# Decode attention on one core: the output projection's weights loaded as 112 + 12 rows instead of 128

## The chip, the cores and the metric

The kernel runs on one core of a Trainium2 chip. The metric is device time in microseconds of one execution, and the median over several runs is given. Besides there is one execution taken by the hardware profiler, whose span runs from the first to the last instruction.

## What is computed

A single token goes through layer norm, attention over a cache of 32,768 keys and values for each of 32 heads, an output projection, a residual, and then a dense block with the activation mish. Everything is in bf16.

```python
B, Sq, D = 1, 1, 512
H, Sk, Dh = 32, 32768, 128          # dense block: F = 1376
q = (layernorm(x) @ wq).reshape(B, Sq, H, Dh).transpose(0, 2, 1, 3)
scores = einsum("bhqd,bhkd->bhqk", q, k_cache) * Dh ** -0.5
o = einsum("bhqk,bhkd->bhqd", softmax(scores), v_cache)
h = x + o.transpose(0, 2, 1, 3).reshape(B, Sq, H * Dh) @ wo      # wo: [4096, 512]
z = layernorm(h) @ w1 + b1
h2 = h + (z * tanh(softplus(z))) @ w2
```

The caches of keys and values are 256 MB each; all weights together are some 11 MB.

## The kernel before

*Order of the loads.* All bulk loads are issued by SP, in one order written out by hand: wq, the keys of head 0, then for each head its keys and the values of the head before it, then `WO` (the output projection's weights wo), the values of the last head `("v", 31)` in five pieces, `WL` (wo's 128 rows for the last head alone), four pieces of w1 and four of w2. Before a load SP waits until the tile it fills has been read (`freed_by`, `done_with`). A load increments a semaphore by 16 when it has landed; `ready[slot]` counts the loads into a slot of the ring, and `ready_wait` turns the count in `fills` into the value to wait for. `start` issues one load.

*Buffers.* `ring` is one large tile of 128 partitions and six slots of 32 KB per partition. One head's keys or values take two slots: 256 positions for each partition, 64 KB. wo takes one slot, viewed as `wo_v` with 32 rows of wo, that is 32 KB, on each partition: partition p holds the rows 32p to 32p+31. Since a head has 128 rows, head h lies on the partitions 4h to 4h+3, and the last head's on 124 to 127.

*One head.* PE transposes 128 x 128 blocks of keys into PSUM (line 685), DVE copies them to `ering` (L691), PE multiplies them with the query (L661). The softmax follows with its maximum and sum over the partitions (`soft_a`, `soft_b`, `soft_exp`, `soft_c`), then PE multiplies the values with the probabilities (L712) and DVE scales the result into a column of `oT` (L720). The heads run as a loop, so that head h's values are used while the keys of head h+1 are transposed.

*The end.* `mid` runs once the second last head is done: the heads' outputs, without the last head's, are transposed into `oX`, whose rows for the last head are zero, and 32 matmuls (L798) contract `oX` with `wo_v`; their results are summed up into `yps` (L803). Then the last head's values arrive in five pieces and PE takes them one after another; `project_last` adds that head's part with `WL` (L779). In `tail` the second layer norm, w1 (L834), mish and w2 (L854) follow, and SP stores the result (L589).

The lines that the change touches are the count of `fills`, the load of wo, and the operands of the 32 matmuls.

Of the kernel before, what the change touches and what calls it, by code (L numbers as in the profile page):

```python
# [13 lines left out]
PE, ACT, DVE, POOL, SP = "pe", "act", "dve", "pool", "sp"  # L14
# [293 lines left out]
def build_kernel(nc, A_x, A_k_cache, A_v_cache, A_wq, A_wo, B_w1, B_b1, B_w2, out):  # L308
    D = A_x.shape[-1]
    Dh = 128  # L310
    HD = A_wq.shape[1]
    H = HD // Dh
# [29 lines left out]
    def sb(shape, dt, name):  # L342
        cm = nc.sbuf_tensor(name, shape, dt)
        t = cm.__enter__()
        allocs.append(cm)
        return t.ap()

    def ps(shape, name, dt=F32):
        cm = nc.psum_tensor(name, shape, dt)
        t = cm.__enter__()  # L350
        allocs.append(cm)
        return t.ap()
# [23 lines left out]
    oX = sb([128, 64], BF16, "oX")  # L376
# [14 lines left out]
    T_f = [ps([128, GT * 64], f"tps{i}") for i in range(NT)]  # L391
# [21 lines left out]
    ready = [sem(f"ready{i}") for i in range(NS)]  # L413
# [3 lines left out]
    s_out = sem("s_out")  # L417
    WQ, WO, WL = ("wq",), ("wo",), ("wl",)
    W1P = [("w1", n) for n in range(KC)]

    W2_J = [0, 4, 8, FJ]
    W2P = [("w2", n) for n in range(len(W2_J))]
# [6 lines left out]
    def pieces(what):  # L429
        kind, h = what  # L430
        if what in (("k", 0), ("v", H - 1)):
            at = CUTS[kind]
        else:
            at = [TPS] if what in (("k", 1), ("v", 1)) else [64] if what == ("k", H - 1) else []
        return list(zip([0] + at, at + [SCOLS]))
# [4 lines left out]
    def uncut(what):  # L440


        kind, h = what
        for r in CUTS[kind]:
            if not cut_at(kind, h, r) and (h == 0 or cut_at(kind, h - 1, r)):
                n = 1
                while h + n < H and not cut_at(kind, h + n, r):
                    n += 1
                yield r, n

    def later_k(h):

        if h == 2:
            for r in CUTS["k"]:
                yield r, sum(1 for n in range(1, H) if n == 1 or not cut_at("k", n, r))

    order = [WQ, ("k", 0)]
    for h in range(1, H):
        order += [("k", h), ("v", h - 1)]
    order += [WO, ("v", H - 1), WL] + W1P + W2P  # L460
    cut_sems = {k: {r: sem(f"cut_{k}_{r}") for r in CUTS[k]} for k in CUTS}

    s_wl = sem("wl")
    s_k1 = sem("k1")
    w1_sems = [sem(f"w1_{n}") for n in range(len(W1P))]
    w2_sems = [sem(f"w2_{n}") for n in range(len(W2P))]
# [6 lines left out]
    def slot_of(what):  # L473
        if what in HOMES:
            return HOMES[what]
        if what[0] in ("w1", "w2"):
            return HOMES[WL]
        return V_HOME if what[0] == "v" else what[1] % 2 * HALVES

    fills = {}  # L480
    for what in order:
        if what[0] in ("k", "v") or what in (WQ, WO):
            fills[what] = 1 + sum(1 for x in fills if slot_of(x) == slot_of(what))

    def ready_wait(what):
        if what == WL:
            return (s_wl, 16)
        return (ready[slot_of(what)], 16 * fills[what])
# [4 lines left out]
    def freed_by(what):  # L493
        if what == WO:
            return done_with("k", H - 2, 0, SCOLS)
        if what[0] == "k" and what[1] > 1:
            return done_with("k", what[1] - 2, 0, SCOLS)
        if what == ("v", 0):
            return [free_name(WQ)]
        return []  # L500

    def tiles_of(what):
        return ring[:, slot_of(what):slot_of(what) + HALVES, :].rearrange("p s (r d) -> p (s r) d", d=Dh)

    def keys_of(cache, h):
        return cache[0, h, :, :].rearrange("(p r) d -> p r d", r=SCOLS)

    wq_v = ring[:, slot_of(("wq",)), :].rearrange("p (k n) -> p k n", k=KC)
    wo_v = ring[:, slot_of(("wo",)), :].rearrange("p (j n) -> p j n", j=32)
# [6 lines left out]
    def done_with(kind, h, r0, r1):  # L516
        if kind == "v":
            return [f"pv{h}_{r1}" if r1 in V_EVENTS else f"pv{h}"]
        return [free_name(("k", h, half)) for half in range(HALVES) if r0 < (half + 1) * TPS and r1 > half * TPS]
# [15 lines left out]
    def program(S):  # L535
        S.home_bytes = HALVES * SLOT * 2
        t_ = nc.tensor
# [6 lines left out]
        def start(dst, src, s):  # L544
            S.dma(SP, lambda: sp.dma_start(dst, src).then_inc(s, 16))  # L545
# [3 lines left out]
        for what in order:  # L549
            slot = slot_of(what)  # L550
            if what == ("k", 1):
                S.stay(SP)
            S.wait(SP, freed_by(what))
            flat = ring[:, slot, :]
            if what[0] == "wq":
                S.wait(SP, ["b1z"])
                start(b1r[0:FJ // 2, :], B_b1[0:FJ * 128].rearrange("(i p) -> i p", i=FJ // 2), s_b1)
                start(b1r[FJ // 2:FJ // 2 + 1, 0:FLAST], B_b1[FJ * 128:F].rearrange("(o p) -> o p", o=1), s_b1)
            elif what[0] == "wo":
                start(flat, A_wo.rearrange("(p j) n -> p (j n)", j=32), ready[slot])  # L560
            elif what == WL:
                start(wol_v, A_wo[(H - 1) * Dh:H * Dh, :], s_wl)
            elif what[0] == "w1":
                k = what[1]
                start(w1_v[:, k, :], B_w1[k * 128:(k + 1) * 128, :], w1_sems[k])
            elif what[0] == "w2":
                n = what[1]
                if n + 1 < len(W2_J):
                    j0, j1 = W2_J[n], W2_J[n + 1]
                    start(w2_v[:, j0:j1, :].rearrange("p (i s) n -> p i (s n)", s=2),  # L570
                          B_w2[j0 * 128:j1 * 128, :].rearrange("(i p s) n -> p i (s n)", p=128, s=2), w2_sems[n])
                else:
                    start(w2_v[0:FLAST, FJ, :], B_w2[FJ * 128:F, :], w2_sems[n])
            else:
                kind, h = what
                rows = keys_of(A_k_cache if kind == "k" else A_v_cache, h)
                for r0, r1 in pieces(what):
                    if kind == "v" and h:
                        S.wait(SP, done_with(kind, h - 1, r0, r1))
                    if what == ("k", 1):  # L580
                        s = ready[slot] if r0 else s_k1
                    else:
                        s = cut_sems[kind][r0] if r0 else ready[slot]
                    start(tiles_of(what)[:, r0:r1, :], rows[:, r0:r1, :], s)


                for r, n in uncut(what) if kind == "v" else later_k(h):
                    S.dma(SP, lambda r=r, n=n: sp.sem_inc(cut_sems[kind][r], 16 * n))
# [194 lines left out]
        def mid():  # L783
            n_b1 = FJ // 2 + 1
            for s in range(2):
                S.step(PE, lambda s=s: t_.matmul(B1_PAIRS[:, s, :], b1r[:, :].rearrange("i (q s) -> i s q", s=2)[:, s, :],
                                                 identb[0:n_b1, 0:FJ // 2], start=True, stop=True),
                       waits=([(s_b1, 32)] if s == 0 else ()))
            S.step(PE, lambda: t_.matmul(B1_REG[:, FJ:FJ + 1], b1r[:, 0:128], identb[0:n_b1, FJ // 2:n_b1], start=True, stop=True),
                   name="b1t")  # L790
            S.step(ACT, lambda: a.copy(b1c[:, :], B1_REG), name="b1c", waits=["b1t"])
            S.step(DVE, lambda: v.transpose(oZ[:, :], oT[:, :]), name="oZ", waits=[f"oev{H - 2}", "oTz"])
            S.step(PE, lambda: t_.matmul(OX_PS, perm[:, :], oZ[:, :], start=True, stop=True), name="oXs", waits=["oZ", "perm"])
            S.step(DVE, lambda: v.tensor_copy(oX[:, 0:32], OX_PS), name="oX", waits=["oXs"])


            for j in range(32):
                S.step(PE, lambda j=j: t_.matmul(T_f[1][32 * (j % 4):32 * (j % 4 + 1), 0:D], oX[:, j:j + 32], wo_v[:, j, :],  # L798
                                                 start=(j < 4), stop=(j >= 28), skip_group_check=True),
                       name=("yrow" if j == 31 else None), waits=(["oX", "oXz", ready_wait(("wo",))] if j == 0 else ()))  # L800
            S.step(DVE, lambda: v.tensor_copy(yrow[:, :], T_f[1][:, 0:D]), name="yrs", waits=["yrow"])
            for c in range(KC):
                S.step(PE, lambda c=c: t_.matmul(yps[:, c:c + 1], yrow[:, c * 128:(c + 1) * 128], sel[:, :],  # L803
                                                 start=(c == 0), stop=False, skip_group_check=True),
                       waits=(["yrs", "sel"] if c == 0 else ()))

        def tail():
# [54 lines left out]
            S.stayed(ACT)  # L862

        S.rounds(H, head, turn, rest, mid, tail)

    log = {}
# [42 lines left out]
```

## Time and profile before

| | |
|---|---|
| median of 3 runs | 1275.37 us (1275.34 to 1275.58) |
| span of the profiled execution | 1273.6 us |
| busy PE / DVE / ACT / POOL | 80% / 56% / 2% / 0% |
| read from HBM | 548.21 MB |
| wo's load, from its issue to its landing | 35.6 us |

The profiled execution's own time beside its span is not listed; the median of the runs lies 1.8 us above the span, which counts from the first to the last instruction only. Shares of busy time are averages over the span. A load's packet is here one partition's row of that load; a window's DMA share and rate count the packets that start in it, so a share can come out a little over 1. "SPq" is SP's queue of issues. In a chain, a time in "DMA" is what passed from the issue to the landing of a load.

### The profile page before, as it was taken

Reading aid. Unit: us, or ns where it says so; the run is one execution under the profiler, and the core shown is the slowest. Engines: PE = TensorE matmul, PEld = TensorE weight load, DVE = VectorE, ACT = ScalarE, POOL = GpSimd, SP = SyncE. Lnnn points to the kernel's source line nnn. Section 1 sums busy time; section 2 is a strip of 40 time slices with the busy share of each in tenths; the row PEclk is TensorE's granted clock in tenths of the full one; section 3 lists DMA queues with packets and bytes.
Section 4 is the critical chain, followed back from the end, with each engine's and each line's share of the span. In section 5 each row is a group of like instructions: output and inputs, shape, how many; then the busy total and the mean of one; then the engine's idle time right before and its main releaser. Section 6 shows DMA issues by size and latency. Waiting matters only on the chain.

```text
span 1273.6 us, 54445 instructions
## 1 busy us (share of the span) xinstructions
PE 1016.5 (80%) x25046; PEld 988.9 (78%) x25046; DVE 715.8 (56%) x1252; ACT 20.6 (2%) x71; POOL 0.9 (0%) x8
## 2 busy tenths in 40 slices
PE   4689877779777789777788777797777897777995
PEld 4689877779777789777788777797777887777994
DVE  2566664456654466644466644566544666445661
ACT  0000000000000000000000000000000000000000
POOL 0000000000000000000000000000000000000000
PEclk9888876778877688867788776787777887677885
DMA  9999999999999999999999999999999999999998
GB/s 403 445 417 437 432 438 434 440 428 428 432 438 430 445 428 428 430 440 428 445 430 428 430 438 430 440 434 428 428 438 432 434 440 428 428 436 434 426 435 353
DMA packets 12350, 548.35 MB, mean 431 GB/s; under 512 B 1360, under 2 KB 1590, under 8 KB 2998
## 3 DMA queue, kind: packets, MB, share of 16 engines
q1 hardware_dynamic: 12340, 548.22, 99.7%
q8 instruction: 8, 0.13, 0.0%
q10 hardware_dynamic: 2, 0.00, 0.0%
HBM read 548.21 MB, written 0.00 MB: 430 GB/s over the span
## 4 chain that ended last, share of the span: by engine, by line
DMA 54%; DVE 23%; PE 18%; issue 2%; SPq 2%; POOL 0%; POOLq 0%
DMA ring<-in_A_k_cache_dram 51%; DVE ering L691 23%; PE ops L712 9%; PE tps L685 6%; DMA ring<-in_A_v_cache_dram 2%; SPq L545 2%; PE sps L661 1%; DMA ring<-in_B_w_dram 1%; PE hlp L736 1%; PE hlp L731 1%; PE hlp L746 0%; PE tps L854 0%; DVE pmax L725 0%; DVE perm L859 0%; DVE gmax L733 0%
## 5 line engine op out<-in xcount | busy, mean ns | idle before, releaser
L685 PE MATMUL tps<-identb,ring 128*128 128x128 bf16 x8192 | 668.3, 232 | 209.4 <-DMA ring<-in_A_k_cache_dram 204.9
L691 DVE COPY ering<-tps 128x1024 bf16<-128x1024 bf16 x1024 | 669.4, 692 | 259.7 <-PE tps L685 258.5
L685 PEld LDWEIGHTS tps<-identb,ring 128*128 x8192 | 522.2, 104 | 212.2 <-issue 212.2
L661 PE MATMUL sps<-qcur,ering 128*128 128x1 bf16 x8192 | 343.7, 164 | 7.7 <-DVE ering L691 6.7
L661 PEld LDWEIGHTS sps<-qcur,ering 128*128 128x128 bf16 x8192 | 309.2, 97 | 10.7 <-DVE ering L691 9.4
L712 PEld LDWEIGHTS ops<-pbuf,ring 128*128 128x128 bf16 x8192 | 226.3, 103 | 24.4 <-issue 15.1
L712 PE MATMUL ops<-pbuf,ring 128*128 128x1 bf16 x8192 | 231.3, 165 | 10.8 <-DMA ring<-in_A_v_cache_dram 8.3
L720 DVE TENSOR_TENSOR oT<-ops,rtotc 128x1 f32 x31 | 5.0, 162 | 109.8 <-PE ops L712 109.8
L733 DVE TENSOR_REDUCE gmax<-hlp 1x1 f32<-1x128 f32 x32 | 8.9, 278 | 67.5 <-PE hlp L731 67.5
L738 DVE TENSOR_SCALAR nbias<-hlp 128x1 f32<-128x1 f32 x32 | 5.1, 158 | 63.4 <-PE hlp L736 63.4
L741 ACT ACTIVATE pbuf<-sps,nbias 128x256 bf16<-128x256 f32 x32 | 15.2, 474 | 1219.9 <-PE ops L712 1166.7
L731 PE MATMUL hlp<-ident,pmax 128*1 128x128 f32 x64 | 17.9, 379 | 5.2 <-issue 5.2
L725 DVE TENSOR_REDUCE pmax<-sps 128x1 f32<-128x256 f32 x32 | 13.6, 425 | 14.3 <-PE sps L661 14.3
L736 PE MATMUL hlp<-gmax,onesmat 1*128 1x1 f32 x64 | 18.5, 356 | 0.4 <-DVE gmax L733 0.4
L736 PEld LDWEIGHTS hlp<-gmax,onesmat 1*128 1x128 f32 x64 | 15.8, 304 | 1.3 <-DVE gmax L733 0.9
L746 PE MATMUL hlp<-esum,onesmat 128*128 128x1 f32 x64 | 12.1, 258 | 4.8 <-issue 1.0
L746 PEld LDWEIGHTS hlp<-esum,onesmat 128*128 128x128 f32 x64 | 9.5, 188 | 7.4 <-issue 7.4
L640 PE MATMUL hlp<-xnT,ring 128*128 128x1 bf16 x128 | 3.6, 165 | 9.2 <-DMA ring<-in_A_wq_dram 9.2
L640 PEld LDWEIGHTS hlp<-xnT,ring 128*128 128x128 bf16 x128 | 3.5, 104 | 9.3 <-issue 9.3
L720 DVE TENSOR_TENSOR oL<-ops,rtotc 128x1 bf16<-128x1 f32 x1 | 0.2, 161 | 14.3 <-PE ops L712 14.3
L731 PEld LDWEIGHTS hlp<-ident,pmax 128*1 128x1 f32 x64 | 2.8, 81 | 5.8 <-issue 5.3
L748 DVE RECIPROCAL rtotc<-hlp 128x1 f32<-128x1 f32 x32 | 5.4, 168 | 2.7 <-PE hlp L746 1.4
(77 smaller groups left out, 40.1 us busy)
## 6 DMA issues: line engine op xcount, KB each, us to landing
ring<-in_A_k_cache_dram SPq DMA_DIRECT2D x3, 4096.0 KB, 40.2
ring<-in_A_v_cache_dram SPq DMA_DIRECT2D x3, 4096.0 KB, 15.3
ring<-in_A_k_cache_dram SPq DMA_DIRECT2D x3, 2048.0 KB, 30.5
ring<-in_A_k_cache_dram SPq DMA_DIRECT2D x1, 6144.0 KB, 44.6
ring<-in_A_wq_dram SPq DMA_DIRECT2D x1, 4096.0 KB, 12.2
ring<-in_A_wo_dram SPq DMA_DIRECT2D x1, 4096.0 KB, 35.6
ring<-in_A_v_cache_dram SPq DMA_DIRECT2D x1, 2048.0 KB, 16.1
ring<-in_B_w_dram SPq DMA_DIRECT2D x4, 344.0 KB, 20.7
```

The costliest lines, as they stand in the source:

```text
L545: S.dma(SP, lambda: sp.dma_start(dst, src).then_inc(s, 16))
L640: S.step(PE, lambda h=h, kc=kc: t_.matmul(Q_REG[:, h:h + 1], wq_v[:, kc, h * Dh:(h + 1) * Dh], xnT[:, 0, kc:kc + 1], start=(kc == 0), stop ...
L661: S.step(PE, lambda r=r: t_.matmul(S_ps[:, col0 + r:col0 + r + 1], ering[:, bg % NE, r, :], qcur[:, :], start=True, stop=True), name=(name ...
L685: S.step(PE, lambda r=r, at=at: t_.matmul(tb[:, r * 128:(r + 1) * 128], key_tile(S, at), identb[:, :], is_transpose=True, start=True, stop ...
L691: S.step(DVE, lambda: v.tensor_copy(ering[:, bg % NE, :, :].rearrange("p r d -> p (r d)"), tb[:, :]), name=f"ev{bg}", waits=[f"trb{bg}"], ...
L712: S.step(PE, lambda r=r: t_.matmul(o_ps[:, 0:1], vt[:, r, :], pbuf[:, r:r + 1], start=(r == 0), stop=(r == SCOLS - 1)), name=(names or Non ...
L725: S.step(DVE, lambda: v.tensor_reduce(pmax[:, :], S_ps[:, 0:SCOLS], AXX, ALU.max), name=f"pmax{h}", waits=[f"qkh{h}"], kind="pmax")
L731: S.step(PE, lambda: t_.matmul(A_REG, pmax[:, :], ident[:, :], start=True, stop=True), name=f"A{h}", waits=[f"pmax{h}", "ident", f"rcp{h - ...
L733: S.step(DVE, lambda: v.tensor_reduce(gmax[:, :], A_REG, AXX, ALU.max), name=f"gmax{h}", waits=[f"A{h}"], kind="gmax")
L736: S.step(PE, lambda: t_.matmul(B_REG, onesm[0:1, :], gmax[:, :], start=True, stop=True), name=f"B{h}", waits=[f"gmax{h}", "consts0"] + ([] ...
L741: S.step(ACT, lambda: a.activation(pbuf[:, :], S_ps[:, 0:SCOLS], ACTF.Exp, bias=nb[:, :], scale=SC, accum_out=esum[:, :]), name=f"exp{h}", ...
L746: S.step(PE, lambda: t_.matmul(C_REG, onesm[:, :], esum[:, :], start=True, stop=True), name=f"C{h}", waits=[f"exp{h}"], kind="C")
```

## The change

The rows of the last head on the partitions 124 to 127, which meet zeros in `oX`, are no longer loaded into `wo_v`. The remaining 124 partitions come in five loads: partitions 0 to 111 with whole rows of 32 KB; partitions 112 to 123 with the first 22 of their 32 rows of wo (22 KB); and the other 10 (10 KB) in three loads of four partitions each. The count of fills grows by four, and the 32 matmuls contract 124 rows.

```diff
+    WO_ROWS = (H - 1) * Dh // 32
+    WO_ALL = WO_ROWS // 16 * 16
+    WO_J = 22
+    WO_STEP = 4
...
+    wo_at = [(0, WO_ALL, 0, 32), (WO_ALL, WO_ROWS, 0, WO_J)]
+    wo_at += [(p, p + WO_STEP, WO_J, 32) for p in range(WO_ALL, WO_ROWS, WO_STEP)]
+    fills[WO] += len(wo_at) - 1
...
             elif what[0] == "wo":
-                start(flat, A_wo.rearrange("(p j) n -> p (j n)", j=32), ready[slot])
+                for p0, p1, j0, j1 in wo_at:
+                    rows = A_wo[32 * p0:32 * p1, :].rearrange("(p j) n -> p j n", j=32)
+                    start(wo_v[p0:p1, j0:j1, :], rows[:, j0:j1, :], ready[slot])
...
-                S.step(PE, lambda j=j: t_.matmul(T_f[1][...], oX[:, j:j + 32], wo_v[:, j, :],
+                S.step(PE, lambda j=j: t_.matmul(T_f[1][...], oX[0:WO_ROWS, j:j + 32], wo_v[0:WO_ROWS, j, :],
```

On SP's queue, at the place between the values of the second last head and the first piece of the last head's values, stood one load. The names are the tile that is filled and the tensor it comes from, and behind them the partitions and the elements of each:

```order
L545 DMA ring<-in_A_k_cache_dram 128x8192
L545 DMA ring<-in_A_k_cache_dram 128x24576
L545 DMA ring<-in_A_v_cache_dram 128x32768
L545 DMA ring<-in_A_wo_dram 128x16384
L545 DMA ring<-in_A_v_cache_dram 128x16384
L545 DMA ring<-in_A_v_cache_dram 128x8192
```

Now five stand there, and nothing else in the queue is moved:

```order
L553 DMA ring<-in_A_k_cache_dram 128x8192
L553 DMA ring<-in_A_k_cache_dram 128x24576
L553 DMA ring<-in_A_v_cache_dram 128x32768
L553 DMA ring<-in_A_wo_dram 112x16384
L553 DMA ring<-in_A_wo_dram 12x11264
L553 DMA ring<-in_A_wo_dram 4x5120 x3
L553 DMA ring<-in_A_v_cache_dram 128x16384
L553 DMA ring<-in_A_v_cache_dram 128x8192
```

The last head's own load of wo's rows, the pieces of w1 and w2 and all other engines keep their order.

More of the change, by code (lines that the diff above doesn't have):

```diff
@@ L419, in build_kernel @@
     W1P = [("w1", n) for n in range(KC)]
+    WO_ROWS = (H - 1) * Dh // 32
+    WO_ALL = WO_ROWS // 16 * 16
+    WO_J = 22
+    WO_STEP = 4
+    assert WO_ROWS * 32 == (H - 1) * Dh and (WO_ROWS - WO_ALL) % WO_STEP == 0
     W2_J = [0, 4, 8, FJ]
@@ L797, in mid @@
             for j in range(32):
-                S.step(PE, lambda j=j: t_.matmul(T_f[1][32 * (j % 4):32 * (j % 4 + 1), 0:D], oX[:, j:j + 32], wo_v[:, j, :],
+                S.step(PE, lambda j=j: t_.matmul(T_f[1][32 * (j % 4):32 * (j % 4 + 1), 0:D], oX[0:WO_ROWS, j:j + 32], wo_v[0:WO_ROWS, j, :],
                                                  start=(j < 4), stop=(j >= 28), skip_group_check=True),
```

## The prediction

> **What bounds the kernel now.** I read the page first (its share of DMA, its queues and its chain), then the DMA queue's own waits and issues, then the last ten microseconds in narrow windows, because the change touches one load near the end.
>
> ```profile
> span 1273.6 us, 54445 instructions
> ...
> q1 hardware_dynamic: 12340, 548.22, 99.7%
> q8 instruction: 8, 0.13, 0.0%
> q10 hardware_dynamic: 2, 0.00, 0.0%
> HBM read 548.21 MB, written 0.00 MB: 430 GB/s over the span
> ## 4 chain that ended last, share of the span: by engine, by line
> DMA 54%; DVE 23%; PE 18%; issue 2%; SPq 2%; POOL 0%; POOLq 0%
> ```
>
> The queue row is the one to see: the loads issued by SP keep 16 DMA engines busy for 99.7% of the span. 430 GB/s over 16 engines is 26.9 GB/s for one, so 10 KB (10,240 B) on one engine is 0.38 us, 22 KB 0.84 us, 32 KB 1.22 us. The chain's 23% of DVE and 18% of PE are work that runs beside a full queue. The span is 1.8 us below the median of the runs, 1275.37; I make the sum as a difference and add it to the median.
>
> The mean says nothing of the end. There the sixteen engines do not stop together:
>
> ```profile
> core 0: us, PE busy (x) PEld busy (x) DVE busy (x) ACT busy (x) POOL busy (x), PEclk, DMA share, GB/s
> 1208.00:1238.00 30.00, 27.82 (x643) 27.13 (x644) 21.89 (x36) 0.26 (x2) 0.00 (x0) 0.84 1.00 432
> 1267.50:1268.25 0.75, 0.75 (x9) 0.58 (x6) 0.40 (x2) 0.00 (x1) 0.00 (x0) 0.50 1.04 381
> 1268.25:1268.50 0.25, 0.12 (x1) 0.00 (x0) 0.01 (x1) 0.21 (x1) 0.00 (x0) 0.50 0.94 336
> 1268.50:1268.75 0.25, 0.00 (x0) 0.00 (x0) 0.21 (x2) 0.00 (x0) 0.00 (x0) 0.50 0.84 229
> 1269.00:1269.75 0.75, 0.35 (x16) 0.31 (x16) 0.31 (x2) 0.00 (x0) 0.03 (x1) 0.50 0.47 179
> 1270.00:1270.25 0.25, 0.25 (x12) 0.25 (x16) 0.00 (x0) 0.00 (x0) 0.00 (x0) 0.50 0.29 98
> 1270.25:1270.75 0.50, 0.44 (x22) 0.14 (x12) 0.00 (x0) 0.00 (x0) 0.00 (x0) 0.50 0.03 8
> ```
>
> The last two columns are the share of the 16 engines and their rate. The share is full to 1268.25, falls to 0.47 by 1269.0, stays there, and is gone by about 1270.4. So about nine engines finish near 1268.65 and about seven near 1270.15: seven are late by some 1.5 us. Where that lateness is from can be seen in the queue rows of two stretches, the first 100 us and the rest up to 1271 us:
>
> ```profile
> q1 hardware_dynamic: 1307, 42.14, 98.7%
> q8 instruction: 7, 0.11, 0.5%
> ...
> q1 hardware_dynamic: 11025, 506.07, 100.0%
> ```
>
> Seven packets of instruction code, 16 KB each, fall into the first 100 us and none into the rest before 1271. Each load lies evenly on the engines and the queue never runs dry, so an engine that once carried such a packet stays late to the end. Seven packets and seven late engines agree (a reading, since no view numbers the engines). The end of the kernel is the end of the late ones:
>
> ```profile
> 1259.74 10.85 DMA ring<-in_B_w_dram
> 1270.59 0.04 issue
> 1270.63 0.54 PE tps L854 x11
> 1271.17 0.02 issue
> 1271.20 0.29 DVE perm L859
> ```
>
> This is the chain in order of time: the last w2 rows land at 1270.59, eleven matmuls, one copy, and the store. What the late engines are spared, the end gains, until the early ones have caught up.
>
> **The change, part by part.**
>
> ```profile
> ring<-in_A_wo_dram SPq DMA_DIRECT2D x1, 4096.0 KB, 35.6
> ...
> 1207.62 0.33 SPq L545 DMA_DIRECT2D ring<-in_A_v_cache_dram  x1
> 1208.05 0.38 SPq L545 DMA_DIRECT2D ring<-in_A_wo_dram  x1
> 1238.20 5.77 SPq L545 DMA_DIRECT2D ring<-in_A_v_cache_dram  x5
> 1244.01 0.43 SPq L545 DMA_DIRECT2D ring<-in_A_wo_dram  x1
> 1244.48 17.07 SPq L545 DMA_DIRECT2D ring<-in_B_w_dram  x8
> ```
>
> *Bytes.* wo goes from 128 rows of 32 KB to 124: 128 KB less, or 0.30 us at 430 GB/s if it were spread evenly. It is not. Before, each engine carries eight rows, 256 KB. Now the load of 112 rows gives each seven, 224 KB. The load of 12 rows gives twelve engines 22 KB. The three loads of 4 rows give four engines each 10 KB. No view says which engines a small load takes, so I bound it.
> (a) Each small load begins at the same first engine: four engines carry 224+22+30 = 276 KB (20 KB more, +0.76 us), eight carry 246 KB (10 KB less, -0.38 us), four carry 224 KB (32 KB less, -1.22 us).
> (b) Small loads go on where the last one stopped: twelve carry 246 KB, four 254 KB, so everyone gets less, -0.38 or -0.08 us.
> With seven late engines, (a) cannot put them all among the four that lose 32 KB, so a late engine is among the eight or among the first four. If all of the first four are early, their +0.76 us fits into the 1.5 us lead, and the end moves with the eight, -0.38 us. If one of the first four is late, the end moves by +0.76 us. I take -0.38: two bounds of three give it, and the packet starts behind the windows, followed from one to the next as far as they could be told apart, show the engines that carry the five bias rows of the start (the only other load of few rows before wo) without the pause of an instruction packet; that is my estimate, since no row groups it. The ends, -0.4 and +0.8, are kept. [...]
>
> *Four more issues on SP.* SP issued wo at 1208.05 and its next load only at 1238.20, when PE had freed the first half of the values. One issue costs 0.38 us here, and two bias loads of five rows and one row took 0.64 us together:
>
> ```profile
> 1.33 0.64 SPq L545 DMA_DIRECT2D b1r<-in_B_b_dram  x2
> ```
>
> So four more, 1.3 to 1.7 us, end by 1210.2, with 28 us in hand: nothing. If that cover were gone they would delay the value loads by 1.7 us. Behind them in SP's queue stand the five pieces of the last values, the last head's wo rows and eight loads of w1 and w2; none moves. The 17 us on the last of these are issues held up by a full queue, not by SP, and the wo packets have left the queue before 1244.
>
> *The wait for wo.* The count that PE waits for now covers five loads.
>
> ```profile
> 1243.82 3.61 PE L798 MATMUL tps<-ring,oX 128*32 128x512 bf16 x32 [0.75 <-DMA ring<-in_A_wo_dram]
> ...
> 1253.45 3.57 PE L712 MATMUL ops<-pbuf,ring 128*128 128x1 bf16 x128 [3.96 <-DMA ring<-in_A_v_cache_dram]
> ```
>
> PE waits 0.75 us for wo at 1243.82, does the 32 projections, and then stands idle 3.96 us for the last values. wo may come 3.9 us later before anything behind it (the reduction over yrow, the last head's values) feels it: cost nothing up to there. The 32 projections contract 124 rows instead of 128 and stream the same 512 columns: nothing, the bound from both sides being their 3.61 us, which lies under that idle time.
>
> *The last values and w1.* They follow wo on the same engines, so their landings move with the late engines too, by the same -0.38 us:
>
> ```profile
> 1263.41 0.59 PE L712 MATMUL ops<-pbuf,ring 128*128 128x1 bf16 x16 [0.71 <-DMA ring<-in_A_v_cache_dram]
> 1267.23 0.51 PE L834 MATMUL sps<-xnT,ring 128*128 128x1 bf16 x11 [0.19 <-DMA ring<-in_B_w_dram]
> 1269.40 1.75 PE L854 MATMUL tps<-ring,actT 128*1 128x128 bf16 x44 [1.02 <-DVE actT L849]
> ```
>
> Each of these waits ends on a load or on what follows from one; the first moves the whole serial tail (layer norm, w1, mish), the last meets the w2 landings. Both branches shift together, so the gain is not lost at 1269.40.
>
> Sum: 0 (issues) + 0 (wait for wo, PE) - 0.38 (late engines) = -0.38 us; 1275.37 - 0.38 = 1275.0 us. Nothing that a comparison would call a change: 0.2% of this kernel, 2.55 us, is about what it can tell from none.
>
> **The rivals.**
>
> *Rows that share a way into the buffer (slower).* All loads of before that carry weight have 128 rows but one, the last of w2, with 96. It runs on the early engines at 1268.1 to 1268.8. In 1268.50:1268.75 a share of 0.84 moved 229 GB/s, 273 for a full share, where 1267.50:1268.25 gives 381/1.04 = 366: packets ran at 0.74 of their speed while that load was there. If a load whose rows lie on few neighbouring partitions is slow, the twelve rows 112 to 123 are the extreme of it. Lower price, 0.74 on the small loads alone: the 52 KB of the first four engines count as 70, +1.4 us, still inside the lead; 22 KB count as 30, so a late engine keeps only -0.1 us: 1275.3. Upper price, if four neighbouring rows get one engine's rate among them: 22 KB takes 3.35 us, each 10 KB 1.52 us; a first engine then needs 7 x 1.22 + 3.35 + 3 x 1.52 = 16.4 us for wo instead of 9.7, +6.7, less its lead of 1.5: +5.2 us, 1280.6. Were the 112 rows hurt as well, at 0.74, another 3.0 us: 1283.6. It decides for slower once the first four engines lose 4 us over their lead and the noise, about 3.3 times their uncontended time on the small rows. For it: that one window. Against it: 1268.25:1268.50, with the same load in flight, moves 336 at 0.94, 357 for a full share, hardly less; the fall came late and briefly. [...]
>
> *A late engine among the first four, or a mild price.* +0.8 us, 1276.1; or no gain at all, 1275.3. For it: seven of sixteen are late, and nothing in a view places them.
>
> *An even spread or more.* If the late engines were those that lose most, the end would move by what the early four allow, 1.5 - 0.76 = 0.74 us: 1274.6. A gain past 0.2% is excluded by the bytes unless the instruction packets fall elsewhere: without any lateness the whole 1.5 us would come, 1273.9, still within.
>
> *It does nothing.* Were the end set by the serial tail alone, 1275.4; against it stands the chain, which ends on the w2 landing.
>
> **How the numbers follow.** Forecast 1275.0, its own range 1274.4 to 1275.3, chance 0.54. Late engine or mild price (1275.3 to 1277.9): 0.17. Shared way: 0.27, spread over 1277.9 to 1284, a little under half of it past 1280.6. Faster by over 0.2%: 0.02. Range 1274.3 to 1280.6, which leaves out about 0.12 above and 0.05 below. Within 0.2%: 0.71; slower 0.27; faster 0.02.
>
> **What would show it.** Right: in the profile after, the share of DMA at the end falls in one step closer to 1270.0; the chain still ends on the w2 rows, landing near 1270.2; PE's wait for wo stays under 1.5 us; four more issues by 1210.2. The rival: during 1241 to 1250 the share stays full while GB/s sinks far under 430, wo lands several us later, PE's waits for the last values grow by as much, and in the last 5 us only about four engines (share 0.25) are busy. Wrong in another way: a changed count or time of the instruction packets, or SP's issues after 1238 starting later.

## The result, and the profile after

The changed kernel takes 1289.47 us (1289.02 to 1290.07), the kernel before 1275.40: 14.1 us more, a ratio of 1.011 (95% interval 1.0096 to 1.0125). The forecast was 1275.0, and its range ended at 1280.6. It is slower by far more than 0.2%.

The loss lies in one place. First the page's span and queue rows of the changed kernel, then stretches of it (the last two columns are the share of the 16 DMA engines and GB/s):

```profile
span 1287.4 us, 54449 instructions
...
GB/s 405 433 429 441 432 432 438 434 426 436 442 424 438 438 428 436 436 432 432 434 438 424 438 442 424 438 438 428 432 436 436 428 434 442 424 438 438 428 256 336
...
q1 hardware_dynamic: 12372, 548.09, 99.7%
```

```profile
core 0: us, PE busy (x) PEld busy (x) DVE busy (x) ACT busy (x) POOL busy (x), PEclk, DMA share, GB/s
1200.00:1230.00 30.00, 29.16 (x708) 28.60 (x706) 20.44 (x34) 0.57 (x2) 0.00 (x0) 0.78 1.00 433
1232.00:1240.00 8.00, 4.41 (x133) 3.90 (x132) 0.50 (x3) 0.00 (x0) 0.00 (x0) 0.60 0.91 205
1240.00:1248.00 8.00, 4.27 (x134) 3.99 (x134) 0.72 (x4) 0.62 (x3) 0.00 (x0) 0.50 1.10 233
1248.00:1256.00 8.00, 0.00 (x0) 0.00 (x0) 0.00 (x0) 0.00 (x0) 0.00 (x0) 0.50 0.94 120
1260.00:1280.00 20.00, 11.38 (x299) 9.80 (x292) 1.81 (x10) 0.07 (x1) 0.00 (x0) 0.59 0.99 408
```

The kernel before, in three of these stretches:

```profile
1232.00:1240.00 8.00, 6.39 (x188) 5.81 (x187) 1.09 (x5) 0.00 (x0) 0.00 (x0) 0.65 0.91 393
1240.00:1248.00 8.00, 6.23 (x118) 3.62 (x115) 1.09 (x4) 0.62 (x3) 0.00 (x0) 0.50 1.05 451
1248.00:1256.00 8.00, 3.82 (x105) 3.74 (x106) 0.34 (x2) 0.00 (x0) 0.00 (x0) 0.71 0.94 402
```

The share says that the engines are busy all the time; the rate beside it says that from 1232 to 1256 they carry a quarter to a half of the 433 GB/s of the first row. That stretch is the load of wo. Before it and after it the rate is as in the kernel before. A busy queue was not a fast queue here: each packet took longer. The trace also keeps the start, length and size of every packet. In the kernel before, a packet of 32 KB took 1.21 to 1.22 us, in wo's load and in the first load of the last values; in the changed kernel 135 of the 240 packets of that size took more than 1.3 us, 2.6 on average and 5.0 at most.

What it does to those who wait, from the issues on SP, the waits, and the end of the chain:

```profile
1207.30 0.33 SPq L553 DMA_DIRECT2D ring<-in_A_v_cache_dram  x1
1207.73 1.82 SPq L553 DMA_DIRECT2D ring<-in_A_wo_dram  x5
1239.85 5.79 SPq L553 DMA_DIRECT2D ring<-in_A_v_cache_dram  x5
1245.68 0.43 SPq L553 DMA_DIRECT2D ring<-in_A_wo_dram  x1
1246.15 28.93 SPq L553 DMA_DIRECT2D ring<-in_B_w_dram  x8
```

```profile
PE tps L808 <- DMA ring<-in_A_wo_dram: 13.2, 1, 13.2
```

```profile
1257.90 3.39 PE L808 MATMUL tps<-ring,oX 124*32 124x512 bf16 x32 [13.18 <-DMA ring<-in_A_wo_dram]
```

```profile
1273.09 11.34 DMA ring<-in_B_w_dram
1284.43 0.04 issue
1284.47 0.52 PE tps L864 x9
1284.99 0.02 issue
1285.01 0.29 DVE perm L869
```

The five issues cost 1.82 us and are over at 1209.55. PE's wait for wo grows from 0.75 to 13.2 us, and its 32 projections start at 1257.90 instead of 1243.82, 14.1 us later. The first issue of the last values slips from 1238.20 to 1239.85, since the values of the head before were slowed too: seven of their 64 KB packets took 3.2 to 3.8 us, where none of that load in the kernel before took more than 2.43. They were the last seven of the load to start, at 1230.60 to 1231.09; the first of wo's rows started at 1231.50, beside them. The eight issues of w1 and w2 are held up for 28.93 us instead of 17.07. The last w2 rows land at 1284.43, 13.8 us later than before.

### The profile page after: what moved, and what is told of

Read it like the earlier page. It is cut to its first block, busy times and chain, and to the rows that moved or that the text cites. A ratio compares the mean times of both kernels' runs of the same rounds, so it can differ in the third digit from the quotient of the medians.

```text
span 1287.4 us, 54449 instructions
## 1 busy us (share of the span) xinstructions
PE 1016.7 (79%) x25046; PEld 990.0 (77%) x25046; DVE 715.8 (56%) x1252; ACT 20.6 (2%) x71; POOL 0.9 (0%) x8
## 4 chain that ended last, share of the span: by engine, by line
DMA 54%; DVE 23%; PE 18%; SPq 3%; issue 2%; POOL 0%; POOLq 0%
DMA ring<-in_A_k_cache_dram 51%; DVE ering L701 23%; PE ops L722 9%; PE tps L695 6%; SPq L553 3%; DMA ring<-in_A_v_cache_dram 2%; PE sps L671 1%; DMA ring<-in_B_w_dram 1%; PE hlp L746 1%; PE hlp L741 1%; PE hlp L756 0%; PE tps L864 0%; DVE pmax L735 0%; DVE perm L869 0%; DVE gmax L743 0%
## 5 line engine op out<-in xcount | busy, mean ns | idle before, releaser
L808 PE MATMUL tps<-ring,oX 124*32 124x512 bf16 x32 | 3.4, 602 | 13.2 <-DMA ring<-in_A_wo_dram 13.2
```

## The experiments

The theories, as they are named in the expectations: A, engines that write neighbouring partitions share one way into the buffer; B, loads of few rows are slow as such; C, the source side in HBM sets the pace. In all kernels only the load of wo, the count of fills where there are several loads, and the rows contracted where that is said differ from the kernel before. Each time is a median of 4 to 11 runs; the kernel before gave 1275.38 to 1275.49 beside them. The intervals reach 1 to 2 us to each side, so what is said of smaller differences goes by the medians alone. `wo_r` is wo seen as 128 rows of 32 KB, `wo_f` the same with each row flat.

### Only the 112 rows

```diff
-start(flat, A_wo.rearrange("(p j) n -> p (j n)", j=32), ready[slot])
+start(wo_v[0:112, :, :], wo_r[0:112, :, :], ready[slot])
```

> Only the load of the 112 rows of wo is kept; the 12 rows after it are left out, and the 32 matmuls contract 112 rows. Theory A (engines that write neighbouring partitions share a way into the buffer; with seven rows for each engine the row groups of two engines overlap): the 112 rows take some 15 us for an engine instead of the 9.7 of the 128 rows, so +5 to +6 us, 1280 to 1281. Theory B (only the loads of 12 and of 4 rows are slow): 0.5 MB less, -1.2 us, 1274.2. Theory C (the source: rows read from HBM at another spacing): as theory A here.

Measured: 1283.01 us (1282.72 to 1283.39), ratio 1.0056 (1.0039 to 1.0073): +7.6, more than the 5 to 6 us that theory A expected, and theory B falls for these rows.

### The same bytes in 128 rows

```diff
+start(wo_v[:, 0:28, :], A_wo[0:112 * 32, :].rearrange("(p j) n -> p j n", j=28), ready[slot])
```

> The same 3.5 MB of wo that the 112 rows hold, read as 128 rows of 28 KB into all 128 partitions (the products are then not those of wo, and the last 12 rows are left out). Theory A and B: the time of the bytes alone, -1.2 us, 1274.2. Theory C (the source): about as the 112 rows. A theory that any change of the row length costs: over 1275.4.

Measured: 1274.21 us (1274.09 to 1274.38), ratio 0.9989 (0.9980 to 0.9999): -1.17, the time of the bytes spared. The two kernels read the same 3.5 MB; between them lie 8.8 us. Their stretches, 112 rows first, then 128:

```profile
1232.00:1240.00 8.00, 4.34 (x132) 3.79 (x132) 0.56 (x4) 0.00 (x0) 0.00 (x0) 0.71 0.89 201
1240.00:1248.00 8.00, 4.41 (x134) 4.12 (x134) 0.72 (x4) 0.62 (x3) 0.00 (x0) 0.50 1.04 250
```

```profile
1232.00:1240.00 8.00, 6.36 (x187) 5.80 (x188) 0.94 (x5) 0.00 (x0) 0.00 (x0) 0.56 0.95 409
1240.00:1248.00 8.00, 6.46 (x121) 3.76 (x118) 1.26 (x4) 0.62 (x3) 0.00 (x0) 0.58 1.04 446
```

About the same share, about half the rate. The engines are as busy, with the same bytes.

### 112 rows and the other 12 in one load

```diff
+start(wo_v[0:112, :, :], wo_r[0:112, :, :], ready[slot])
+start(wo_v[112:124, :, :], wo_r[112:124, :, :], ready[slot])
```

The 32 matmuls contract 124 rows here.

> 112 rows, and the other 12 with their full 32 KB in one load; no loads of four rows. Theory A: the 12 rows lie on three groups of four partitions, so 32 KB for an engine take four times 1.22 us, 4.9 us: about 3.5 to 5 us more than with the 112 rows alone, 1284 to 1286, and 3 to 5 us below the changed kernel's 1289.5. Theory B: 1279 to 1281, of which nothing is from the 112 rows.

Measured: 1290.01 us (1289.12 to 1290.72), ratio 1.0112 (1.0095 to 1.0129). The 12 rows add 7.0 us to the 112, more than the 3.5 to 5 us expected. The changed kernel, at 1289.47, overlaps with it: the split into 22 KB and three times 10 KB bought nothing that can be measured, where theory A had expected 3 to 5 us (a miss in the other direction too: the loads of four rows were not the dear ones).

### Two halves of 64 rows

```diff
+start(wo_v[0:64, :, :], wo_r[0:64, :, :], ready[slot])
+start(wo_v[64:128, :, :], wo_r[64:128, :, :], ready[slot])
```

> All of wo in two loads, partitions 0 to 63 and 64 to 127, four rows for each engine. [...] Theory A with groups of four partitions and no more sharing: each engine has a group of its own, no loss, 1275.4. Theory C (the source): 1275 to 1276.

Measured: 1287.40 us (1286.51 to 1288.17), ratio 1.0089 (1.0072 to 1.0106). All of wo, all engines busy (share 0.90 to 1.01), and +12.0 us. So groups of four with no more sharing, for which 1275.4 was expected, do not account for it. The wo stretches of this kernel ran at half rate:

```profile
1232.00:1240.00 8.00, 3.84 (x111) 3.32 (x112) 0.94 (x4) 0.00 (x0) 0.00 (x0) 0.57 0.90 184
1240.00:1248.00 8.00, 5.17 (x161) 4.87 (x158) 0.72 (x4) 0.62 (x3) 0.00 (x0) 0.50 1.01 213
```

### Sixteen rows, four partitions apart or in a row

Each of the four kernels here loads 9 KB for all 128 partitions into a free part of another slot, and then four times 16 rows of 32 KB; half of wo is left out. The first, second and fourth differ in the partitions that are written at once, the third from the second in the source rows.

```diff
+for s in range(4):
+    start(wo_v[32 + s:96:4, :, :], wo_r[32 + s:96:4, :, :], ready[slot])
```

> wo's load is replaced by 9 KB for each of 128 partitions (into a free part of another slot, to keep the queue filled) and four loads of 16 rows of 32 KB, which lie four partitions apart (32, 36, ... 92, then 33, 37, ... and so on). Together they fill partitions 32 to 95; the rest of wo is left out. 3.28 MB instead of 4.19, so -2.1 us by bytes. [...] Theory B (loads of few rows are slow as such): as the next one.

Measured: 1273.40 us (1273.27 to 1274.35), ratio 0.9985 (0.9975 to 0.9994): -2.07, the time of the bytes spared. These loads of 16 rows were not slow as such. Theory B falls.

```diff
+    start(wo_v[32 + 16 * s:48 + 16 * s, :, :], wo_r[32 + 16 * s:48 + 16 * s, :, :], ready[slot])
```

> The same partitions 32 to 95, the same rows and bytes, but each of the four loads fills 16 partitions in a row. Theory A: four engines share one way, each load takes 4.85 us instead of 1.21, +14.6 - 2.1 us, 1287 to 1288. Theory B: as the one before it.

Measured: 1287.62 us (1284.67 to 1288.09), ratio 1.0088 (1.0071 to 1.0104): 14.2 us between two kernels that move the same bytes to the same partitions in the same number of loads. The stretch of wo, four apart and then in a row:

```profile
1232.00:1240.00 8.00, 6.40 (x187) 5.76 (x186) 1.09 (x5) 0.00 (x0) 0.00 (x0) 0.67 1.03 423
1240.00:1248.00 8.00, 6.46 (x126) 3.67 (x123) 1.26 (x4) 0.62 (x3) 0.00 (x0) 0.50 0.95 406
```

```profile
1232.00:1240.00 8.00, 6.48 (x190) 5.93 (x191) 1.08 (x5) 0.00 (x0) 0.00 (x0) 0.65 1.25 235
1240.00:1248.00 8.00, 2.51 (x82) 2.24 (x79) 0.57 (x3) 0.62 (x3) 0.00 (x0) 0.50 0.91 131
```

Next, the same destination with the other kernel's source rows:

```diff
+    start(wo_v[32 + 16 * s:48 + 16 * s, :, :], wo_r[32 + s:96:4, :, :], ready[slot])
```

> As the one before it, 16 partitions in a row, but each load reads the source rows of the first of these kernels, 128 KB apart instead of 32 KB (the products are then not those of wo). Theory A: the source is of no matter, 1287 to 1288. Theory C (the source side sets the pace): 1273.3, as the loads four partitions apart.

Measured: 1286.58 us (1285.85 to 1287.63), ratio 1.0085 (1.0068 to 1.0102). The source's spacing makes no difference that its interval shows. Theory C falls.

```diff
+    start(wo_v[s:64:4, :, :], wo_r[s:64:4, :, :], ready[slot])
```

> [...]

Measured: 1279.76 us (1279.62 to 1280.11), ratio 1.0034 (1.0021 to 1.0046). Four apart again, but on partitions 0 to 63: 6.4 us over the 1273.40 us of partitions 32 to 95. So it is not the distance between the rows alone that counts, but also which partitions they are on. In theory A's words, as an estimate from the 1.21 us of an undisturbed 32 KB packet: with two engines to a way each of the four loads would take 1.21 us longer, 4.85 us in all, and with four engines to a way 14.6. Measured are 6.4 on partitions 0 to 63 and 14.2 for 16 in a row, alike in order and roughly in size. Which partitions share a way is not shown: no run separates a pairing of partitions from a limit of the lower 64 partitions as a whole.

### The small loads without the 112 rows

Both kernels load 128 rows of 28 KB, then 12 rows of 9 KB and three times 4 rows of 4 KB; in the first the rows lie next to each other, on partitions 112 to 123, in the second four apart.

```diff
+start(w12[112:124, 11776:11776 + 4608], wo_f[112:124, 0:4608], ready[slot])
+for s in range(3):
+    start(wo_v[112 + 4 * s:116 + 4 * s, 28:32, :], wo_r[112 + 4 * s:116 + 4 * s, 28:32, :], ready[slot])
```

> The small loads without the 112 rows: the 128 rows of 28 KB (1274.2 us alone), then 12 rows of 9 KB on partitions 112 to 123 (into a free part of another slot) and three loads of 4 rows of 4 KB on 112 to 115, 116 to 119, 120 to 123; wo's products are not those of the reference. Theory A: four engines share one engine's rate, 36 KB take 1.37 us instead of 0.34, and each load of four rows 0.61 instead of 0.15. A late engine among the twelve loses 1.4 us, one that owns such a way up to 1.95, the first four 3.2 less their lead of 1.5: 1275.6 to 1276.2. Theory B (few rows are slow as such): the same as the next kernel.

```diff
+start(w12[32:80:4, 11776:11776 + 4608], wo_f[112:124, 0:4608], ready[slot])
+for s in range(3):
+    start(wo_v[32 + s:48:4, 28:32, :], wo_r[112 + 4 * s:116 + 4 * s, 28:32, :], ready[slot])
```

> As the one before it, with the same numbers of loads, rows and bytes and the same source rows, but the 12 rows lie four partitions apart (32, 36, ... 76), and each load of 4 rows too (32, 36, 40, 44 and so on). Theory A: no way is shared, 9 KB more for a late engine, +0.34 us: 1274.5 to 1274.6. Theory B: as the one before it.

Measured: 1277.28 us (ratio 1.0015, 1.0006 to 1.0024) next to each other, 1274.47 (0.9992, 0.9983 to 1.0001) apart. Apart came out as expected, +0.26 over the 128 rows of 28 KB alone (0.15 when each is taken against the kernel before beside it). Together cost 2.8 us for 156 KB, 1.1 us beyond the upper end of theory A's estimate, in which four engines share one engine's rate. After the 28 KB rows, in 1240 to 1248, the rate is 289 together and 430 apart:

```profile
1240.00:1248.00 8.00, 5.00 (x112) 3.46 (x113) 0.57 (x3) 0.62 (x3) 0.00 (x0) 0.50 0.99 289
```

```profile
1240.00:1248.00 8.00, 6.46 (x119) 3.68 (x116) 1.26 (x4) 0.62 (x3) 0.00 (x0) 0.50 1.00 430
```

### What the spared bytes are worth

```diff
+start(wo_v[:, 0:31, :], A_wo[0:124 * 32, :].rearrange("(p j) n -> p j n", j=31), ready[slot])
```

> What the bytes of the last head's rows are worth at best: wo's 31 heads as 128 rows of 31 KB, 1 KB less for each partition (the products are then not those of wo, since a partition no longer begins with a whole 32nd of it). Theory A and the reading that the end follows the late engines: 8 KB less for each engine, -0.30 us, 1275.1.

Measured: 1275.18 us (1274.98 to 1276.19) beside 1275.49, ratio 0.9997 (0.9988 to 1.0006). By the medians 0.31 us, as worked out; the interval holds no change. That is about what leaving out the last head's rows has to give where every engine is spared the same.

## Why the prediction was wrong

*What bounds the kernel: right.* By the medians, 8 KB less for each engine came out as -0.31 us, 32 KB as -1.17 (1.22 by the rate), 9 KB more for each of twelve engines, in rows four apart, as +0.26. The end followed the bytes for each engine nearly one to one, as the forecast's -0.38 assumed; that it is the late engines whose bytes count was not tested apart. The seven instruction packets lie in the first 100 us again:

```profile
q1 hardware_dynamic: 1307, 42.14, 98.5%
q8 instruction: 7, 0.11, 0.4%
```

*The four issues and the 32 matmuls: right.* The issues ended at 1209.55 and held nobody up; the matmuls took 3.39 us instead of 3.61.

*The step that failed: the bytes.* The sum gave each engine 224 KB at 1.22 us for 32 KB in both (a) and (b). That is the price in a load of 128 rows, where no packet was drawn out (1.21 to 1.22 us in wo's load before); it was carried over to 112 rows without a row that shows such a load. With 112 rows 8.8 us were lost against the same bytes in 128 rows, shown by the first two experiments; that engines then meet on a way is theory A's account of it. What the changed kernel adds to the 112 rows alone is 6.5 us, of which the 384 KB are worth 0.9 and 5.6 are loss: -1.17 + 8.8 + 0.9 + 5.6 = +14.1. This sum closes by construction, since its terms are differences of the same times.

*A second account, from the lengths of the packets.* It does not rest on those differences. The first column has what each kernel lost against a kernel that moves the same bytes with no packet drawn out. The second takes each packet from about 1190 us on, and how much longer it took than packets of its size take where none is drawn out (for 22 and 10 KB an estimate from the rate); the sum is divided by 16 engines, less the same sum of the kernel compared with, which is 0.1 to 0.5 us.

| kernel | lost, us | packets longer, us for each engine |
|---|---|---|
| the changed kernel (0.30 us of bytes spared) | 14.4 | 14.1 |
| 112 rows | 8.8 | 8.9 |
| 112 and 12 rows (0.30 us of bytes spared) | 14.9 | 13.9 |
| 64 and 64 rows | 12.0 | 12.5 |
| 16 in a row | 14.2 | 14.1 |
| 16 in a row, other source rows | 13.2 | 13.9 |
| 16 four apart, partitions 0 to 63 | 6.4 | 6.4 |
| small loads next to each other | 2.8 | 2.7 |

So the time lost at the end is, within some 1 us, the time by which packets were drawn out.

*One sum beside it is off.* In (b), with small loads that go on where the last one stopped, the three loads of four rows would fall on three different groups of engines: eight engines would carry 256 KB, four 246 and four 234, so not everyone would get less. It did no harm, since (a) is what the trace shows: on four engines a 22 KB packet is followed by three of 10 KB, each within 3 ns of the end of the one before.

*The wait for wo: wrong as its consequence.* "Cost nothing up to 3.9 us" was not put to the test, since wo came some 14 us later. It was not the wait that counted all the same: the last values and w1 and w2 stood behind wo on the same engines, and PE's longest wait for the last values stayed at 3.88 us, against 3.96 before.

*The rival named it and undersized it.* Rows that share a way into the buffer had 0.27. Its upper price for the small loads, +5.2 us, was near the 5.6 they lost in fact. The term behind it, one engine's rate for four neighbouring rows among them, is shown by no run for such rows alone; shown are 14.2 us lost by 16 rows in a row against 16 four apart, and 2.8 by small loads next to each other against the same four apart. For the 112 rows it had 3.0 us, from a factor of 0.74; they lost 8.8. Of its signs the full share at a low rate and the late wo came true; waits for the last values that grow by as much did not. Even 1283.6 was too low, and the range had been cut below it. The weighing went wrong at one window: 1268.25:1268.50 was taken as evidence against, because the load of 96 rows ran there hardly slowed (336 GB/s at a share of 0.94). That load has 96 KB, 6 KB for each engine on average. Why its first quarter of a microsecond ran freely is not shown by a run here; it was too small a load to price one of 224 KB by.

*The spread at the end* was to be one fall of the share, and by the rival four engines (share 0.25) alone in the last microseconds. Instead the share falls over some two microseconds:

```profile
1282.00:1282.50 0.50, 0.23 (x2) 0.00 (x0) 0.22 (x2) 0.21 (x1) 0.00 (x0) 0.50 0.82 279
1282.50:1283.00 0.50, 0.00 (x0) 0.00 (x0) 0.42 (x3) 0.00 (x0) 0.21 (x1) 0.50 0.69 256
...
1283.25:1283.50 0.25, 0.25 (x12) 0.25 (x16) 0.00 (x0) 0.00 (x0) 0.00 (x0) 0.50 0.41 148
```

That fits the third experiment, where full 32 KB rows did as badly as the split ones: others were held up too, not just the engines that carry the loads of four rows. The packets say the same: 21 of the 32 KB packets took more than 3.2 us, where with the 112 rows alone none took more than 2.55.

*Open.* Which rows of a load of 112 an engine carries is not shown, and whether a late engine is among the four with the most small rows was not settled; neither is needed for the verdict. A version that spares the 0.3 us with the right products would need the heads' outputs in another order; none was built, and no run that keeps wo's products beats the kernel before.

## What to carry to other kernels

Where a queue of loads bounds the time, weigh a smaller load by the partitions that are written at the same moment, not by its bytes: 128 KB less cost 14 us here, and 16 rows in a row instead of four apart 14.2. Load all 128 partitions with shorter rows rather than fewer partitions: the same 3.5 MB of wo took 1274.21 us as 128 rows of 28 KB and 1283.01 as 112 rows of 32 KB. If it must be few, spread them: here 16 rows four apart on partitions 32 to 95 lost nothing, on 0 to 63 they lost 6.4 us. In a profile, read the DMA share and GB/s side by side: a full share at half the rate (0.91 and 205 GB/s from 1232 to 1240) was here the sign of packets drawn out, to 5.0 us at most instead of 1.22.

## What the runs showed that was not expected

The loss is larger than a fair division in theory A would make it. With two engines to a way and each 32 KB packet at twice 1.21 us, an estimate from that length alone, the four loads of 16 rows would lose 4.85 us and the two loads of 64 rows 9.7; lost were 6.4 on partitions 0 to 63, and 12.0. The small loads next to each other cost 2.8 us where fair shares, by the estimate put down before, gave 1.1 to 1.7. The packets show where the rest lies. On partitions 0 to 63 the first 64 packets of 32 KB took 2.45 us on average, about twice the 1.22 us, and some 4.9 us more for each engine. Another 1.8 us are in the neighbours: 24 of the 9 KB rows issued ahead took up to 0.75 us instead of 0.35, and 25 of the 32 KB packets behind were drawn out too. Sixteen in a row seem to come out at the fair price of four engines to a way, 14.2 against the estimate of 14.6, but in part by luck: the first 64 packets took 3.67 us on average and not four times 1.22, which is 9.8 us more for each engine, and the neighbours add 4.6.

The harm thus reaches back as well as forward. In the changed kernel the values issued before wo, untouched by the change, were taken into use 1.6 us later.

```profile
1207.30 28.29 DMA ring<-in_A_v_cache_dram
1235.60 0.05 issue
1235.64 1.86 PE ops L722 x64
```

This is the chain of the changed kernel where PE takes those values up, at 1235.64. The kernel before did so at 1234.02:

```profile
1207.62 26.35 DMA ring<-in_A_v_cache_dram
1233.97 0.05 issue
1234.02 1.84 PE ops L712 x64
```
